# A fused attention and mixture kernel: a second conversion tile, PSUM banks shared 2-3-3, and other order around two units of the second mixture

## The chip, the cores and the metric

The kernel runs on one core of one Trainium2 chip. The core has a matrix engine (TensorE, in the profile PE; its weight loads are the row PEld), three elementwise engines (VectorE or DVE, ScalarE or ACT, GpSimd or POOL), and a sync engine (SP) that here only issues transfers. Each engine works through its own instructions in order and waits on semaphores. The metric is the device time of one execution in microseconds (us); lower is better.

## The reference

All of it is float32. Attention (plain softmax at a quarter of the resolution plus a band of seven keys) gives 2304 rows of 512; then follow two dense blocks:

```python
def _moe_ref(x, w1, w2, w3, w_out):      # 512 -> 768 -> 512
    h = np.maximum(np.maximum(x @ w1, x @ w2), x @ w3)
    return h @ w_out

def _moe2_ref(x, w_a, w_b, w_out):       # 512 -> 1536 -> 512
    a = x @ w_a
    b = x @ w_b
    return a * b @ w_out
```

The weights arrive as float64 bit patterns. This case is about the second block, called the second mixture here.

## The kernel before

**Tiling.** The 2304 rows are six blocks of 384 (`TB`). Every float32 operand is kept as a high part and a low part, and a product is three passes (high by high, low by high, high by low). The second mixture takes its 1536 columns in six chunks `c` of 256 and its rows in three pairs `p` of blocks. A *unit* is one (c, p). The loop over units runs (0,0), (0,1), (1,0), ... (5,1) and then (0,2) to (5,2): units 0 to 11, then 12 to 17. Unit 11, (5,1), is called `turn` in the code.

**A unit** (`m2_unit`, line 878) computes `a` and `b` (index j = 0, 1) for two column tiles and two blocks by a scheme of seven products in place of eight, in the order 1, 2, 6, 5, 7, 4, 3. Each product is done for j = 0 and j = 1, with six matmuls of 384 columns each (`prod`, line 827). Products 1, 6, 7 and 4 accumulate in the two "ua" banks, with a copy out by ACT in between (`snap`, tile `sn`); product 2 takes two "ub" banks, product 5 two more, on which product 3 then accumulates. `m2_done` (line 853) adds a bank to a copy (DVE): for j = 0 into `ca`, for j = 1 into `g`, and multiplies `g` by `ca`. `m2_parts` splits `g` into `gh` (ACT cast, line 874) and `gl` (POOL subtraction, line 875), one step of the unit later.

**Output.** `m2_o` (line 917) multiplies the `g` of the unit before by `w_out`: six steps of six matmuls of 512 columns, each into an "o" bank (`bank`, line 607), each followed by an addition into `acc` (DVE, line 944; in chunk 0 a copy by ACT, line 942) and, in the last chunk, by a store. The main loop sets these *o steps* between the products with `o(n)`: one after product 6, one after 5, two after 7, two after 4; in unit 11 all six stand after product 4. PSUM has eight banks: "ua" 2, "ub" 4, "o" 2.

**Operands.** `sform(p, ...)` (line 681) makes the seven left operands of a pair from the sums of the first block: for each a cast on ACT (line 691), a subtraction (line 694) on DVE where its number is in `SUB_DVE`, else on POOL, and between them differences on DVE (`less`, line 700, in place). It is a generator in lane 0. Pair 0 and 1 are made around the end of the first mixture. The sums of blocks 4 and 5 (pair 2) are written to DRAM in unit 0 (`spill`), and `refill` (line 1056) reads them back into two "w6" tiles at the start of unit 10; `sform(2, ...)` is queued at the start of unit 11.

**Weights.** `convert_steps` (line 463) turns 512 columns of float64 bits into float32 on DVE (lines 471, 474, 479, 481, 488) and ACT (478), with tiles `ce` and `cm` of one buffer each (`CB = 1`). For the rows of `w_out` the result stays in `cm`, from which `split2` (line 764) takes it to `wo` (ACT 768, POOL 770). `conv2_in` and `conv2_out` are generators in lane 1. All split weights are also stored to DRAM, and units 12 to 17 load them again (`load2`, line 818), some on SP's queue and some on ACT's.

**Order.** From the end of attention on the order on each engine is the program's (`manual_schedule`). `tick` runs the lanes, lane 0 first; a lane stops at a yielded tuple such as ("x", 4) until the main loop has put it into `opened`. In an engine's queue a transfer stands where the program issues it. The last lines of the loop's body, where unit n loads `w_out` rows again, are:

```python
        o(6 if turn else 2)
        while prev_o:
            part(one_o)
        opened.add(("o", n - 1))
        if turn:
            load2(nc.scalar, 0, 0, 3)
        elif p == 2:
            load2(nc.scalar, c, 1, 3)
            load2(nc.scalar, c + 1, 0, 3)
        step(3)
```

Of the kernel before, what the change touches and what calls it, by code (L numbers as in the profile page):

```python
# [38 lines left out]
W2B = 4  # L39
SNB = 5  # L40

SUB_DVE = (0, 2, 4)

SUM_ACT = (0, 1, 2, 3, 4, 6, 7, 8, 9, 10, 13, 14, 15)
NORM_POOL = (0, 1, 2, 3, 4, 5, 6, 7, 8, 9, 10, 11, 13, 14, 15)
# [4 lines left out]
def attn_moe_kernel(  # L50
# [397 lines left out]
    W = 12 * P  # L448
    NP_ = 512
    raw, wt = {}, {}  # L450

    def load_piece(key, srcs):

# [9 lines left out]
    def convert_steps(key, w=None):  # L463

        r = raw.pop(key)
        lo, hi = r[:, :, 0], r[:, :, 1]
        top = r.rearrange("p n w -> p (n w)").bitcast(U16).rearrange("p (n w) -> p n w", w=4)[:, :, 3]
        e = rawp.tile([P, NP_], U16, tag="ce", name="ce", bufs=CB)
        m = rawp.tile([P, NP_], U32, tag="cm", name="cm", bufs=CB)
        s16, f = e.bitcast(I16), m.bitcast(F32)  # L470
        nc.vector.tensor_scalar(  # L471
            out=e, in0=top, scalar1=0x7FF0, scalar2=None, op0=ALU.bitwise_and
        )
        nc.vector.tensor_scalar(  # L474
            out=m, in0=hi, scalar1=0x000FFFFF, scalar2=0x00100000, op0=ALU.bitwise_and, op1=ALU.bitwise_or
        )
        yield
        nc.scalar.activation(out=s16, in_=e, func=AF.Relu, bias=ebias, scale=8.0)  # L478
        nc.vector.scalar_tensor_tensor(out=f, in0=lo, scalar=2.0**-32, in1=m, op0=ALU.mult, op1=ALU.add)  # L479
        yield  # L480
        nc.vector.scalar_tensor_tensor(  # L481
            out=e, in0=top, scalar=0x8000, in1=e, op0=ALU.bitwise_and, op1=ALU.bitwise_or
        )
        yield
        out, i0, i1 = f if w is None else w, f, e.bitcast(BF16)
        if w is not None and len(w.shape) == 3:
            i0, i1 = (x.rearrange("p (a b) -> p a b", a=w.shape[1]) for x in (i0, i1))
        nc.vector.scalar_tensor_tensor(out=out, in0=i0, scalar=2.0**-20, in1=i1, op0=ALU.mult, op1=ALU.mult)  # L488
        yield f
# [116 lines left out]

    def bank():
        if 2 in psp_:
            return psp_[2].tile([P, 512], F32, tag="o", name="ps_m", bufs=2)
        return bk("d", "ps_m")  # L610

    def m1_p(c, blk, j):
# [40 lines left out]
            else:  # L653
                nc.vector.tensor_tensor(out=a, in0=ps, in1=a, op=ALU.add)  # L654

    late = {}

# [20 lines left out]
    def sform(p, s0, s1):  # L681


        b11, b21, b12, b22 = (s[:, k * YH : (k + 1) * YH] for s in (s0, s1) for k in range(2))
        n = [0]

        def part(i, w):
            t = ys_tile(p, n[0])
            h = t[:, :HK].rearrange("p k t -> p (k t)")
            l = t[:, HK:].rearrange("p k t -> p (k t)")  # L690
            nc.scalar.copy(h, w)
            yield
            eng = nc.vector if n[0] in SUB_DVE else nc.gpsimd
            eng.tensor_tensor(out=l, in0=w, in1=h.bitcast(F32), op=ALU.subtract)
            n[0] += 1
            ys[p, i] = t
            yield

        def less(o, a, b):
            nc.vector.tensor_tensor(out=o, in0=a, in1=b, op=ALU.subtract)  # L700

        if p == 1:
            yield ("x", 4)
        yield from part(1, b11)
        less(b11, b12, b11)
        yield
        yield from part(2, b21)
        yield from part(5, b11)
        less(b12, b22, b12)
        less(b11, b22, b11)  # L710
        yield
        if p == 0:
            yield ("x", 2)
        if p == 1:
            yield ("x", 5)
        yield from part(7, b12)
        yield from part(6, b11)
        less(b21, b21, b11)
        yield
        yield  # L720
        if p == 1:
            yield ("x", 6)
        yield from part(4, b21)
        if p == 0:
            yield ("x", 3)
        yield from part(3, b22)
# [126 lines left out]
    def m2_done(c, p, j, i, b, ps, t):  # L853

        if j == 0:
            o = ca[i, b] = late["p"].tile([P, TB], F32, tag="ca", name="ca", bufs=2)
            if t is None:
                nc.scalar.copy(o, ps)
            else:
                nc.vector.tensor_tensor(out=o, in0=ps, in1=t, op=ALU.add)  # L860
            return
        g = late["p"].tile([P, TB], F32, tag="g", name="g", bufs=3)
        if t is not None:
            nc.vector.tensor_tensor(out=g, in0=ps, in1=t, op=ALU.add)  # L864
        nc.vector.tensor_tensor(out=g, in0=ps if t is None else g, in1=ca.pop((i, b)), op=ALU.mult)  # L865
        fresh.append((c, p, i, b, g))
# [11 lines left out]
    def m2_unit(c, p):  # L878


        def bank_u(tag, n):
            return psp_[2].tile([P, 512], F32, tag=tag, name="ps_u", bufs=n)[:, :TB]

        A, E, T2 = [None] * 2, [None] * 2, [None] * 2
        T1 = [None] * 2
        for j in range(2):
            A[j] = bank_u("ua", 2)
            prod(A[j], c, p, j, 1, True)
            T1[j] = snap(A[j])
            yield  # L890
        for j in range(2):
            b = bank_u("ub", 4)
            prod(b, c, p, j, 2, True)
            m2_done(c, p, j, 0, 0, b, T1[j])
            yield
        for j in range(2):
            prod(A[j], c, p, j, 6, False)
            T2[j] = snap(A[j])
            yield
        for j in range(2):  # L900
            E[j] = bank_u("ub", 4)
            prod(E[j], c, p, j, 5, True)
            yield
        for j in range(2):
            prod(A[j], c, p, j, 7, False)
            m2_done(c, p, j, 1, 1, E[j], snap(A[j]))
            yield
        for j in range(2):
            prod(A[j], c, p, j, 4, False)
            m2_done(c, p, j, 1, 0, A[j], None)  # L910
            yield
        for j in range(2):
            prod(E[j], c, p, j, 3, False)
            m2_done(c, p, j, 0, 1, E[j], T2[j])
            yield
# [154 lines left out]
    for n, (c, p) in enumerate(units):  # L1070
        unit = m2_unit(c, p)
        turn = (c, p) == (NC2 - 1, 1)

        nxt = c + 1 if p == 2 else 0 if turn else NC2
        if n == 0:
            lanes[1].extend(conv2(*x) for x in conv2_order(0, 0))
        elif p < 2:
            lanes[1].extend(conv2(*x) for x in conv2_order(c, p))
        if (c, p) == (NC2 - 1, 0):
            back = list(refill())  # L1080
        if turn:
            lanes[0].append(sform(2, *back))

        def part(f):
            old, fresh[:] = fresh[:], []
            f()
            for x in old:
                m2_parts(*x)

        def step(m, k_=1):  # L1090
            for _ in range(m):
                part(lambda: next(unit, None))
                tick(k_)

        def one_o():
            while prev_o and next(prev_o[0], StopIteration) is StopIteration:
                prev_o.pop(0)

        def o(m):
            for _ in range(m):  # L1100
                part(one_o)
                tick(2)

        step(4)
        if n == 0:
            m1_o(*last)
            spill(4)
            spill(5)
            acc_ctx.close()
            xps["e"] = ctx.enter_context(tc.tile_pool(name="xpe", bufs=2, side="right", reuse_waits="tile"))  # L1110
            opened.add(("x", 6))
        else:
            prev_o = [m2_o(*u) for u in prev_u]
        if p == 2:
            if c == 0:
                load_in(1, 0)
            load_in(c + 1, 2)
        step(2)
        if p == 1 and c < NC2 - 1:
            opened.add(("a", n, 0))  # L1120
        if turn:
            load2(nc.sync, 0, 0, 0)
        elif p == 2:
            load_in(c + 1, 1)
        if not turn:
            o(1)
        step(2, 2)
        if not turn:
            o(1)
        step(2)  # L1130
        if not turn:
            o(2)
        step(2)
        if p == 1 and c < NC2 - 1:
            opened.add(("a", n, 1))
        if turn:
            load2(nc.scalar, 0, 1, 0)
            load_in(0, 1)
            load_in(0, 2)
        elif p == 2:  # L1140
            load_in(c + 2, 0)
# [10 lines that stand above are left out]
        prev_u = [(c, 2 * p), (c, 2 * p + 1)]  # L1152
# [33 lines left out]
```

## Time and profile before

| | |
|---|---|
| median of 3 runs | 895.41 us (894.58 to 904.71) |
| the profiled execution | 895.55 us, span 893.3 us |
| mean granted TensorE clock | 0.974 |
| PE busy | 853.1 us, 95% of the span |
| PE weight loads | 795.0 us, 89% |
| DVE busy | 620.9 us, 70% |
| ACT busy | 346.4 us, 39% |
| POOL busy | 381.6 us, 43% |
| second mixture, units 0 to 17 | from 449.92 us to the end |

The span goes from the first to the last instruction of the profiled execution; its time has 2.25 us more around it. Times in the rows are counted from the span's start. Matmuls are pipelined: a row's duration covers its latency, so the distance between starts tells how fast they go. The granted clock is 1.00 at 2.4 GHz and 0.50 at 1.2 GHz.

### The profile page before, as it was taken

The numbers are of one execution on the slowest core, as the hardware profiler recorded it, in microseconds if no ns is written. First come the engines' busy times: TensorE is split into PE (matmuls) and PEld (weight loads), VectorE is DVE, ScalarE is ACT, GpSimd is POOL, SyncE is SP. The second block draws the span as 40 slices with busy tenths as digits, with TensorE's granted clock in tenths as the row PEclk, the third lists the DMA queues.
The fourth block names the chain that finished last, engine by engine and source line by source line (L and its number), as shares of the span: only waits on it lengthen the run. The fifth ranks groups of instructions, "written<-read, shape, count | busy, mean of one in ns | idle before, by whom it ended". The sixth has DMA issues, their size and how long they took to land.

```text
span 893.3 us, 14751 instructions
## 1 busy us (share of the span) xinstructions
PE 853.1 (95%) x5590; PEld 795.0 (89%) x5590; DVE 620.9 (70%) x1101; ACT 346.4 (39%) x791; POOL 381.6 (43%) x388
## 2 busy tenths in 40 slices
PE   5899889999999999999987899999999989999998
PEld 4778779999999999999986898898889989999996
DVE  5989996754675685757869788989898564334444
ACT  4576565545422232322333553334334242322221
POOL 5777776644232232323545454455444333111111
PEclk9599989999999999999999999999999999999999
DMA  8875754311121130211315444444443348755612
GB/s 186 187 147 120 141 120 91 77 31 38 50 71 48 38 97 31 77 77 72 130 70 187 167 177 177 156 175 176 150 180 113 135 144 333 254 212 212 212 48 95
DMA packets 125110, 116.22 MB, mean 130 GB/s; under 512 B 81392, under 2 KB 107760, under 8 KB 125040
## 3 DMA queue, kind: packets, MB, share of 16 engines
q1 hardware_dynamic: 120720, 97.98, 36.3%
q10 hardware_dynamic: 4320, 17.30, 5.3%
q8 instruction: 44, 0.72, 0.3%
q14 instruction: 26, 0.21, 0.1%
HBM read 80.66 MB, written 34.60 MB: 129 GB/s over the span
## 4 chain that ended last, share of the span: by engine, by line
PE 73%; DVE 19%; issue 3%; ACT 2%; DMA 2%; POOL 1%; SPq 0%; DVEq 0%; ACTq 0%
PE ps_m L602 44%; PE ps_u L836 19%; PE ps_s L303 3%; DVE ce L471 2%; DVE cm L474 2%; PE ps_av L416 2%; DVE ce L481 2%; DVE g L865 2%; PE ps_sd L295 2%; PE ps_tl L391 1%; DVE F L488 1%; DVE cm L479 1%; DVE acc L944 1%; DVE g L864 1%; PE ps_ud L402 1%
## 5 line engine op out<-in xcount | busy, mean ns | idle before, releaser
L602 PE MATMUL ps_m<-xh,w 128*128 128x384 f32 x864 | 174.8, 340 | 1.4 <-DVE t L631 1.4
L875 POOL TENSOR_TENSOR gl<-g,gh 128x384 fp32r<-128x384 f32 x72 | 75.4, 1048 | 212.9 <-ACT gh L874 197.6
L602 PEld LDWEIGHTS ps_m<-xh,w 128*128 128x128 f32 x864 | 152.1, 190 | 2.4 <-DVE t L631 1.6
L836 PE MATMUL ps_u<-xh,w 128*128 128x384 f32 x720 | 135.7, 338 | 2.4 <-DVE ca L860 1.7
L602 PE MATMUL ps_m<-wo,gh 128*128 128x512 f32 (+1 forms) x436 | 131.2, 395 | 6.3 <-DVE acc L944 3.0
L836 PEld LDWEIGHTS ps_u<-xh,w 128*128 128x128 f32 x720 | 127.9, 190 | 5.5 <-DVE ca L860 2.0
L836 PE MATMUL ps_u<-xl,w 128*128 128x384 f32 x648 | 121.8, 336 | 3.6 <-DVE g L865 1.7
L836 PEld LDWEIGHTS ps_u<-xl,w 128*128 128x128 f32 x648 | 113.9, 188 | 7.0 <-DVE g L865 2.0
L602 PEld LDWEIGHTS ps_m<-wo,gh 128*128 128x128 f32 x436 | 79.9, 188 | 23.7 <-DVE acc L944 6.5
L944 DVE TENSOR_TENSOR acc<-ps_m,acc 128x512 f32<-128x512 f32 (+1 forms) x91 | 61.5, 682 | 56.4 <-PE ps_m L602 56.3
L602 PE MATMUL ps_m<-xl,w 128*128 128x384 f32 x432 | 94.3, 336 | 0.0
L874 ACT CAST gh<-g 128x384 fp32r<-128x384 f32 x72 | 37.0, 514 | 138.1 <-DVE g L865 120.6
L631 DVE TENSOR_TENSOR t<-ps_m,t 128x384 f32<-128x384 f32 x72 | 39.9, 555 | 68.6 <-PE ps_m L602 54.9
L848 ACT COPY sn<-ps_u 128x384 f32<-128x384 f32 x108 | 50.0, 478 | 80.2 <-PE ps_u L836 68.6
L602 PE MATMUL ps_m<-hh,wo 128*128 128x384 f32 x288 | 73.7, 337 | 3.6 <-DVE acc L654 2.1
L602 PEld LDWEIGHTS ps_m<-xl,w 128*128 128x128 f32 x432 | 76.3, 188 | 0.5 <-issue 0.4
L637 POOL TENSOR_TENSOR hl<-t,hh 128x384 fp32r<-128x384 f32 x36 | 36.4, 1010 | 79.2 <-ACT hh L636 77.8
L602 PE MATMUL ps_m<-wo,gl 128*128 128x512 f32 (+1 forms) x218 | 67.8, 392 | 0.0
L481 DVE SCALAR_TENSOR_TENSOR ce<-raw,ce 128x512 uint16<-128x512 uint16 x60 | 50.5, 842 | 18.1 <-ACT ce L478 18.1
L654 DVE TENSOR_TENSOR acc<-ps_m,acc 128x384 f32<-128x384 f32 x120 | 61.4, 552 | 1.1 <-PE ps_m L602 1.1
L478 ACT ACTIVATE ce<-ce,ebias 128x512 int16<-128x512 uint16 x60 | 43.5, 725 | 40.5 <-DVE ce L471 40.3
L860 DVE TENSOR_TENSOR ca<-ps_u,sn 128x384 f32<-128x384 f32 x54 | 29.9, 554 | 40.7 <-PE ps_u L836 21.0
(123 smaller groups left out, 1423.6 us busy)
## 6 DMA issues: line engine op xcount, KB each, us to landing
dw<-w SPq DMA_DIRECT2D x24, 768.0 KB
raw<-in_moe_w_dram SPq DMA_DIRECT2D x18, 512.0 KB
raw<-in_moe_w_out_dram SPq DMA_DIRECT2D x18, 512.0 KB
w<-dw SPq DMA_DIRECT2D x12, 768.0 KB
w<-dw ACTq DMA_DIRECT2D x12, 768.0 KB
dw<-wo SPq DMA_DIRECT2D x12, 512.0 KB
wo<-dw ACTq DMA_DIRECT2D x12, 512.0 KB
vr<-in_v_dram SPq DMA_DIRECT2D x16, 288.0 KB
```

The lines of the kernel that those rows point to most:

```text
L478: nc.scalar.activation(out=s16, in_=e, func=AF.Relu, bias=ebias, scale=8.0)
L481: nc.vector.scalar_tensor_tensor(out=e, in0=top, scalar=0x8000, in1=e, op0=ALU.bitwise_and, op1=ALU.bitwise_or)
L602: nc.tensor.matmul(ps, lhs[a], rhs[b], start=(i == 0), stop=(i == n - 1))
L631: nc.vector.tensor_tensor(out=t, in0=ps, in1=cur["t"], op=ALU.max)
L637: nc.gpsimd.tensor_tensor(out=l, in0=t, in1=h.bitcast(F32), op=ALU.subtract)
L654: nc.vector.tensor_tensor(out=a, in0=ps, in1=a, op=ALU.add)
L836: nc.tensor.matmul(ps, w[:, a, slot, kk], y[:, b * HK + kk], start=start and i == 0, stop=i == 3 * HK - 1, skip_group_check=not start,)
L848: nc.scalar.copy(t, ps)
L860: nc.vector.tensor_tensor(out=o, in0=ps, in1=t, op=ALU.add)
L874: nc.scalar.copy(h, g)
L875: nc.gpsimd.tensor_tensor(out=l, in0=g, in1=h.bitcast(F32), op=ALU.subtract)
L944: nc.vector.tensor_tensor(out=a, in0=ps, in1=a, op=ALU.add)
```

## The change

It does five things; all else keeps its order.

- Conversion: once the pool `late` exists (after attention), every other piece takes its `ce` and `cm` from that pool, so that there are two of each. The buffers of `g` there go from three to two.
- Banks: "ub" has 3 instead of 4, "o" 3 instead of 2; "ua" keeps 2.
- `SUB_DVE` is now set for each pair; for pair 1 only part 2 stays on DVE, parts 0 and 4 go to POOL.
- `sform(2, ...)` is queued in unit 10. It is let go in three steps: ("x", 7) in unit 10 before product 6, ("x", 8) there after product 7, ("x", 9) at the start of unit 11.
- Unit 17 has its o steps two after product 6, two after 5, two after 7.

```diff
-SUB_DVE = (0, 2, 4)
+SUB_DVE = {0: (0, 2, 4), 1: (2,), 2: (0, 2, 4)}
...
+    late, late_n = {}, [0]
...
-        e = rawp.tile([P, NP_], U16, tag="ce", name="ce", bufs=CB)
-        m = rawp.tile([P, NP_], U32, tag="cm", name="cm", bufs=CB)
+        late_n[0] += "p" in late
+        pl = late["p"] if late_n[0] % 2 else rawp
+        e = pl.tile([P, NP_], U16, tag="ce", name="ce", bufs=CB)
+        m = pl.tile([P, NP_], U32, tag="cm", name="cm", bufs=CB)
...
-            return psp_[2].tile([P, 512], F32, tag="o", name="ps_m", bufs=2)
+            return psp_[2].tile([P, 512], F32, tag="o", name="ps_m", bufs=3)
...
-            eng = nc.vector if n[0] in SUB_DVE else nc.gpsimd
+            eng = nc.vector if n[0] in SUB_DVE[p] else nc.gpsimd
...
         if p == 1:
             yield ("x", 4)
+        if p == 2:
+            yield ("x", 7)
         yield from part(1, b11)
...
             yield ("x", 5)
+        if p == 2:
+            yield ("x", 8)
         yield from part(7, b12)
...
             yield ("x", 6)
+        if p == 2:
+            yield ("x", 9)
         yield from part(4, b21)
...
-        g = late["p"].tile([P, TB], F32, tag="g", name="g", bufs=3)
+        g = late["p"].tile([P, TB], F32, tag="g", name="g", bufs=2)
...
-            b = bank_u("ub", 4)
+            b = bank_u("ub", 3)
...
-            E[j] = bank_u("ub", 4)
+            E[j] = bank_u("ub", 3)
...
         if (c, p) == (NC2 - 1, 0):
-            back = list(refill())
+            lanes[0].append(sform(2, *refill()))
         if turn:
-            lanes[0].append(sform(2, *back))
+            opened.add(("x", 9))
...
+        if (c, p) == (NC2 - 1, 0):
+            opened.add(("x", 7))
         step(2)
...
-        if not turn:
-            o(1)
+        end = n == len(units) - 1
+        o(0 if turn else 2 if end else 1)
         step(2, 2)
-        if not turn:
-            o(1)
+        o(0 if turn else 2 if end else 1)
         step(2)
-        if not turn:
-            o(2)
+        if (c, p) == (NC2 - 1, 0):
+            opened.add(("x", 8))
+        o(0 if turn else 2)
         step(2)
```

## Rows read from the trace of the kernel before

**Rows 1.** Windows by stage: from:to, length, busy us (instructions) per engine, PEclk, DMA share, GB/s.

```profile
449.92:502.95 53.03, 43.26 (x217) 39.34 (x217) 38.79 (x59) 23.35 (x44) 27.53 (x22) 0.97 0.38 138
502.95:692.39 189.44, 186.44 (x962) 170.71 (x962) 167.68 (x258) 77.41 (x150) 93.07 (x81) 1.00 0.46 165
692.39:715.38 22.99, 22.99 (x121) 21.38 (x121) 13.41 (x21) 6.46 (x13) 7.42 (x7) 1.00 0.36 130
715.38:742.49 27.11, 24.70 (x123) 22.86 (x123) 17.32 (x23) 10.05 (x18) 11.93 (x8) 0.94 0.53 191
742.49:880.10 137.61, 137.61 (x720) 127.96 (x719) 53.77 (x90) 34.47 (x72) 24.38 (x24) 1.00 0.54 194
880.10:893.30 13.20, 9.25 (x44) 7.18 (x43) 5.42 (x9) 0.51 (x1) 1.01 (x1) 0.94 0.38 141
```

**Rows 2.** Timeline, from unit 5 into 6: start, duration, engine, line, operation, [idle before].

```profile
571.62 2.25 PE L836 MATMUL ps_u<-xh,w 128*128 128x384 f32 x12
573.71 2.26 PE L836 MATMUL ps_u<-xl,w 128*128 128x384 f32 x12
...
573.59 0.55 DVE L860 TENSOR_TENSOR ca<-ps_u,sn 128x384 f32<-128x384 f32 x1
```

**Rows 3.** Timeline of PE, units 0 and 1; in brackets the idle time before.

```profile
457.51 0.62 PE L602 MATMUL ps_m<-hh,wo 128*128 128x384 f32 x2 [2.09 <-DVE acc L654]
...
470.42 2.39 PE L836 MATMUL ps_u<-xh,w 128*128 128x384 f32 x12 [1.67 <-DVE ca L860]
...
477.26 1.31 PE L836 MATMUL ps_u<-xl,w 128*128 128x384 f32 x6 [1.68 <-DVE g L865]
...
494.21 0.73 PE L602 MATMUL ps_m<-wo,gh 128*128 128x512 f32 x2 [2.37 <-ACT acc L942]
```

**Rows 4.** Timelines of DVE and POOL, the end of the first mixture and unit 0.

```profile
445.29 2.49 DVE L700 TENSOR_TENSOR acc<-acc 128x768 f32<-128x768 f32 x1
...
456.04 0.95 DVE L694 TENSOR_TENSOR xl<-acc,xl 128x768 fp32r<-128x768 f32 x1
...
468.74 0.43 DVE L474 TENSOR_SCALAR cm<-raw 128x512 uint32<-128x512 uint32 x1 [7.78 <-POOL wo L770]
...
445.07 1.89 POOL L694 TENSOR_TENSOR xh<-acc,xh 128x768 fp32r<-128x768 f32 x1 [3.51 <-ACT xh L691]
```

**Rows 5.** Windows around three pauses of PE; the column after POOL is its clock.

```profile
459.00:461.00 2.00, 2.00 (x8) 2.00 (x7) 1.76 (x3) 0.00 (x0) 0.00 (x0) 0.50 0.23 95
...
490.00:494.00 4.00, 1.84 (x9) 1.24 (x7) 3.86 (x8) 1.03 (x2) 0.00 (x0) 1.00 0.56 201
...
728.00:730.00 2.00, 1.62 (x5) 1.62 (x6) 1.01 (x2) 1.44 (x3) 1.82 (x1) 0.50 0.00 0
```

**Rows 6.** Waits of PEld, units 2 to 9 (total, times, longest); POOL's group from the page.

```profile
PEld ps_m L602 <- DVE acc L944: 6.2, 10, 0.9
...
L875 POOL TENSOR_TENSOR gl<-g,gh 128x384 fp32r<-128x384 f32 x72 | 75.4, 1048 | 212.9 <-ACT gh L874 197.6
```

**Rows 7.** Timelines of SP, PE, ACT and a window's traffic, units 10 and 11.

```profile
694.79 1.47 SPq L1059 DMA_DIRECT2D w<-y  x2
...
701.00:702.00 1.00, 1.00 (x8) 1.00 (x7) 0.00 (x0) 0.00 (x0) 0.00 (x0) 1.00 0.53 221
...
703.53 2.24 PE L836 MATMUL ps_u<-xl,w 128*128 128x384 f32 x12
...
727.12 0.83 ACT L691 CAST xl<-w 128x768 fp32r<-128x768 f32 x1 [3.50 <-DVE w L700]
...
728.38 3.73 PE L836 MATMUL ps_u<-ys,w 128*128 128x384 f32 x12 [2.41 <-ACT sn L848]
```

**Rows 8.** Timeline of the last unit: ACT, its queue of transfers, and PE.

```profile
876.28 0.51 ACT L874 CAST gh<-g 128x384 fp32r<-128x384 f32 x1 [1.25 <-DVE g L865]
...
878.15 0.33 ACTq L822 DMA_DIRECT2D wo<-dw  x1
...
881.51 0.47 PE L602 MATMUL ps_m<-wo,gh 128*128 128x512 f32 x1 [0.84 <-DMA wo<-dw]
```

More of the change, by code (lines that the diff above doesn't have):

```diff
@@ L654, in m1_o @@
                 nc.vector.tensor_tensor(out=a, in0=ps, in1=a, op=ALU.add)
-    late = {}
     HK = NK // 2
```

## The prediction

> **What bounds the kernel now.** I read the page first: TensorE (PE) is busy for 95% of the span, and in its forty slices the 9s break only at the very start, near slice 20, near slice 32 and at the end. So I cut the span into stages with the table of windows [rows 1]; its borders are starts of units in the chain of work that ended last. A unit here is one (c, p) of the second mixture.
>
> Six units on the third pair last 137.61 us, 22.94 each, with PE busy throughout and the clock at 1.00 [rows 1]. That is the floor of a unit. Twelve matmuls of 384 columns take 2.09 us from start to start (571.62 to 573.71 [rows 2]), 0.174 each; a unit has 84 of them, 14.6 us, so its 36 matmuls of the output, six "o" steps of six, are 22.94 - 14.6 = 8.3 us, 1.39 a step.
>
> Against that floor the stages lose: units 0 and 1 last 53.03 and should need 14.6 (unit 0 has no o steps) + 2.1 (the last `m1_o`, 12 matmuls) + 22.94 = 39.6, so 13.4 is lost; units 2 to 9 last 189.44 against 183.5, 5.9 lost; unit 10 nothing; unit 11 27.11, 4.2 lost; units 12 to 17 nothing; after them come the last six o steps (8.3) in 13.20. All the change can win is here, about 23.5 us, 2.6%. Everything before 449.92 keeps its instructions.
>
> **The start (units 0 and 1).** Four rows of PE's timeline show what it waited for [rows 3]: a bank that VectorE (DVE) had not read (2.09 us), DVE's `ca` (1.67), DVE's `g` (1.68), and a bank that ScalarE (ACT) had not copied (2.37). Behind them [rows 4]:
>
> - Third "o" bank and the moved subtraction. At 457.51 the third of four outputs waited for the first's addition, which DVE made after a 0.95 us subtraction of `sform(1)` (456.04). The diff sends that one to POOL (`SUB_DVE[1]` keeps only part 2), so the addition moves to about 456.05 and ends near 456.65; the third output has a bank of its own, runs to 455.8, and the fourth waits 0.85 instead of the third 2.09: 1.24 won. The pause at 457.51 was followed by a clock of 0.50, the 1.2 GHz level, in 459 to 461 [rows 5]: about 1.0 us lost, which I count as won.
> - The further conversion tile. DVE stood 7.78 us, to 468.74, because the one `cm` tile was still being read by POOL's split (`wo`, L770). With pieces alternating between two `ce`/`cm` pairs, DVE goes on at about 461, and `ca` waits only for its product. The 1.67 at 470.42 goes. The 1.68 at 477.26 stays mostly: DVE works through conversion, `ca`, `g` in one line there, and that line just starts sooner. I take 0.9 of it and its neighbours.
> - At 494.21 the fourth o step waited for ACT's copy of the second, itself behind a conversion step. With three banks it needs the first's copy, long done: 2.37 gone, but the next product needs a `sn` copy from that same ACT line, about 0.5 later: 1.87 won.
> - The price. Part 0's subtraction, also moved to POOL, reads `b11`, which DVE's L700 then overwrites: DVE must now wait for POOL's 1.89 us. At 445.29 an L700 beside POOL's subtraction (445.07) took 2.49 instead of 0.95. Bounds: 0 if DVE's own 0.95 saved pays for it, 1.2 if the L700 also sits out POOL's next subtraction. I take the middle, 0.6.
>
> Start: 1.24 + 1.0 + 1.67 + 0.9 + 1.87 - 0.6 = 6.1 us won. Bounds 2.0 (the last bank wait alone) and 9.0 (all 13.4 but 0.85, 0.5 and some 3 of DVE's line).
>
> On that price the Trainium skill (SBUF — State Buffer, Who interferes with whom) says that a DVE instruction with two SBUF inputs and a POOL instruction that reads SBUF exclude each other for the whole instruction. The 2.49 us row agrees; by that rule alone the price is the full 1.2 and the sum 0.6 us higher.
>
> **Units 2 to 9.** The PE loads waited 6.2 us in ten waits, all for `acc` (L944) to free an "o" bank [rows 6]. With three banks the fifth o step needs the bank of the second, not of the third, whose addition lies more than 2.8 us (two steps) earlier; the longest wait was 0.9. I take 5.4 of 5.9; bounds 2.5 and 5.9, the low one if shorter units let DVE fall behind. The third bank comes from "ub", four to three. Now the second bank of product 2 waits for `ca` of the preceding unit's product 3: in the tightest unit that is read at 573.59 and takes 0.56, while product 2's second half starts 3.1 us after 573.71, less 0.8 for the removed waits: 1.9 us of room [rows 2]. `g` from three to two buffers: a buffer comes back two results later, at the closest (product 4 to the next unit's 2) after three products and two o steps, 3 x 2.09 + 2.78 = 9.05 us, and POOL's split that frees it takes 1.05 [rows 6]; it would have to start 8 us late to matter: nothing.
>
> **Units 10 and 11 (the turn).** In unit 11 PE waited 2.41 us for an ACT `sn` that stood behind `sform(2)`'s copy, itself 3.50 late for DVE [rows 7]; the clock then was 0.50 [rows 5], and 12 matmuls took 3.73. That is the 4.2. The change puts five of the seven operands into unit 10, where DVE is busy 13.41 of 22.99 us [rows 1]; unit 11 keeps two, both subtracted on POOL. What is new: the first ACT copy now wants the refill from DRAM from the middle of product 6 on. The refill is issued at 694.79 as before and the DMA traffic thins out between 701 and 702 [rows 7]; ACT and all queued behind it (the `sn` of product 6's second half, then `gh`) stand until about 701.6, and the second half of product 7 (703.53 plus half of 2.09) needs that `sn` near 704.6. Copy 0.84 and `sn` 0.48 end at 702.9. So 1.7 us of room, and DVE, late too, has a third bank to lean on. I take 3.7 won; bounds 1.5 and 4.2.
>
> **The last unit.** Its o steps go 2-2-2 instead of 1-1-2-2, so the last two precede product 4 (12 matmuls) instead of following it. That moves the issue of the last `wo` load, which the program puts on ACT's queue behind the `gh` cast of product 4. Before, ACT was ready at 876.28 and the load went at 878.15, when the last o step freed the slot; it landed 3.36 us later, at 881.51, and PE waited 0.84 for it [rows 8]. Now the slot is free earlier, but product 4 ends two o steps (2.78) later, so `gh` starts at 879.06 and the load goes then: 0.91 later, and nothing covers it, since PE reaches its own end of products at the same time. So +0.9; PE then stands about 1.8 us. Such a pause cost the clock at 728.38 but a longer one, 2.37, did not: 490 to 494 shows 1.00 [rows 5]. I add 0.4 of a possible 1.5: +1.3, bounds +0.9 and +2.4.
>
> On the clock the Trainium skill (TensorE: Matmul & The Clock Gate, What's actually happening) says that its watching window runs free, so that equal pauses may cost or not. These rows agree; by it the end is +0.9 or +2.4, never between.
>
> **Sum.** -6.1 - 5.4 - 3.7 + 1.3 = -13.9 us. The profiled execution took 895.55 us (span 893.3 and 2.25 around it): 881.65. The median shown is 895.41, 0.14 lower: 881.5 us. Against 895.41 that is -1.55%; about 2% (17.9 us, below 877.5) is what a measurement of this kernel tells from no change.
>
> **Rivals.**
> - *The start's waits only move.* Speaks for it: after 468.74 DVE has hardly an idle row. If `g` and `sn` hold PE as long as before, the start wins 2.0: 885.6, up to 888 if clock losses stay.
> - *DVE becomes the bound in units 2 to 9.* It is busy 167.68 of 189.44 us there [rows 1], and shorter units leave it 91%. If the steady gain is only 0.5: 886.4. Against: its idle rows before o steps show that it catches up in each second unit.
> - *The turn's stall moves to unit 10*, ACT standing for the refill. If the refill lands after 704, product 7 waits and the turn wins 0 to 1.5: 883.7 to 885.2.
> - *Slower: the "ub" banks.* With POOL taking more and DVE converting beside it, DVE's lag at product 3 passes the 1.9 us of room and the wait recurs in all eight units. It outweighs the 13.9 once each waits 1.74 us, a lag of 3.65. With a lag of 4.5 it is 8 x 2.6 = 20.8 - 13.9, 902.3. Against: the tightest lag row already is that of a DVE in a long backlog, and it still leaves the room.
> - *Everything at its bound*: -9.0 - 5.9 - 4.2 + 0.9 = -18.2, 877.2.
>
> **How the numbers follow.** Forecast 62% (878 to 886); start's waits move 14%; DVE the bound 9%; turn 6%; "ub" banks 5%, of it 3 in 100 beyond 913.3 (2% slower: a lag near 5.9); all bounds 4%. Low 877.5 and high 890.0 leave out the last, the "ub" case and the worst mixtures of the three middle ones (all three at once: -2.0 - 0.5 - 1.5 + 2.4, 893.8). Faster by over 2%: 0.05; within: 0.92; slower: 0.03.
>
> **What would show it.** Right: no 7.78 us row at `cm`, unit 2 starting near 497 instead of 502.95; no PE wait on L944 between units 2 and 9, with 46.0 us per two units; unit 11 near 23.3 us without a 0.50 clock and L691 rows in unit 10 near 701; PE waiting about 1.8 us for `wo` before its last o steps. Wrong: PE waits on `ca` or `g` at product 2 or 5 in each unit (the banks), an ACT row idle past 704 for the refill, or units 2 to 9 still over 23.4 us.

## The result and the profile after

The kernel after takes 889.76 us at the median of 20 runs, the kernel before, timed beside it, 896.98. The ratio is 0.9905 with a 95% interval of 0.9879 to 0.9932: some 8.5 us won (6.1 to 10.9), where 13.9 were forecast. The ratio is that of the fast executions alone: six of the 20 after, 894.58 us and more at a lower granted clock, are left out of it, while the medians are of all. The profiled execution took 889.42 us, its span is 887.6.

The windows of the kernel after, cut at the starts of units 0, 2, 10, 11 and 12 and of the last o steps (from:to, length, then busy us and instructions of PE, PEld, DVE, ACT, POOL, then PEclk, DMA share, GB/s):

```profile
451.73:498.02 46.29, 41.36 (x216) 37.85 (x217) 40.15 (x59) 22.62 (x44) 29.36 (x21) 1.00 0.43 154
498.02:685.45 187.43, 185.06 (x961) 171.01 (x961) 174.07 (x258) 78.00 (x152) 95.38 (x82) 1.00 0.46 166
685.45:709.63 24.18, 23.52 (x122) 21.25 (x122) 19.77 (x24) 8.79 (x16) 10.08 (x8) 1.00 0.38 142
709.63:734.35 24.72, 23.65 (x121) 21.23 (x121) 13.99 (x22) 7.51 (x15) 10.27 (x8) 1.00 0.62 218
734.35:872.35 138.00, 138.00 (x722) 128.33 (x721) 53.79 (x90) 34.35 (x72) 23.99 (x24) 1.00 0.53 190
872.35:887.60 15.25, 10.34 (x43) 8.06 (x42) 5.43 (x9) 0.51 (x1) 1.42 (x2) 0.89 0.37 136
```

In [rows 1] two borders lie one matmul off: unit 12 of the kernel before starts at 742.31, not 742.49, and its last o steps at 880.27, not 880.10. Cut at its start, the last stretch of the kernel before is:

```profile
880.27:893.30 13.03, 9.08 (x43) 7.01 (x42) 5.42 (x9) 0.51 (x1) 1.01 (x1) 0.94 0.38 137
```

By these starts a unit on the third pair takes 137.96 / 6 = 22.99 us; that is the floor, not the 22.94 of the prediction, and eight units take 183.9. The table takes the same starts for both kernels (us):

| stage | before | after | won | forecast |
|---|---|---|---|---|
| units 0 and 1 | 53.03 | 46.29 | 6.74 | 6.7 (and a price of 0.6, which falls ahead of unit 0) |
| units 2 to 9 | 189.44 | 187.43 | 2.01 | 5.4 |
| units 10 and 11 | 49.92 | 48.90 | 1.02 | 3.7 |
| units 12 to 17 | 137.96 | 138.00 | -0.04 | 0 |
| last o steps | 13.03 | 15.25 | -2.22 | -1.3 |

The start came out as forecast, two stages won far less, and the end lost more. What precedes unit 0 took 1.81 us longer in this execution; that length differs from run to run (unit 0 starts between 444.62 and 454.11 in most of the runs below), so I compare stages.

The timeline of PE, units 0 and 1 of the kernel after, its waits in brackets; these answer [rows 3]:

```profile
451.73 2.37 PE L843 MATMUL ps_u<-xh,w 128*128 128x384 f32 x12 [1.24 <-DVE acc L657]
458.92 0.61 PE L605 MATMUL ps_m<-hh,wo 128*128 128x384 f32 x2 [1.17 <-DVE acc L657]
...
474.15 1.31 PE L843 MATMUL ps_u<-xl,w 128*128 128x384 f32 x6 [1.71 <-DVE g L872]
...
490.96 2.35 PE L843 MATMUL ps_u<-ys,w 128*128 128x384 f32 x12 [0.83 <-ACT sn L855]
```

The wait of 2.09 us for the "o" bank is 1.17 (0.85 forecast), the 1.67 for `ca` is gone with DVE's 7.78 us idle row [rows 4], the 1.68 for `g` stands as it was, and in place of the 2.37 for ACT's copy there are 0.83 for the `sn` copy behind it (0.5 forecast). The clock was 1.00 throughout.

In units 2 to 9 the waits of PE changed their name. The waits table of the kernel after in that stage (total us, times, longest), against 6.2 us for `acc` in [rows 6]:

```profile
PEld ps_u L843 <- ACT sn L855: 3.3, 3, 1.1
PE ps_u L843 <- ACT sn L855: 2.4, 3, 0.8
...
PEld ps_m L605 <- DVE acc L951: 0.4, 2, 0.2
```

Cut by unit, the windows of the kernel after show where (unit 4, then unit 5; 6 and 8 are like 4, 7 and 9 like 5):

```profile
544.11:567.10 22.99, 22.99 (x121) 21.32 (x121) 21.00 (x29) 8.24 (x16) 13.00 (x11) 1.00 0.53 206
567.10:591.21 24.11, 23.30 (x122) 21.34 (x122) 23.03 (x38) 10.31 (x20) 10.50 (x10) 1.00 0.39 132
```

Unit 4 is at the floor of 22.99. Unit 5 is over it by 1.1 us, and DVE is busy 23.03 of its 24.11 us, with 38 instructions against 29 in unit 4. At its border with unit 4 the chain is this (timelines of DVE, ACT and PE of the kernel after):

```profile
570.08 1.15 DVE L872 TENSOR_TENSOR g<-g,ca 128x384 f32<-128x384 f32 x1
...
571.31 0.51 ACT L881 CAST gh<-g 128x384 fp32r<-128x384 f32 x1 [2.33 <-DVE g L872]
571.73 0.85 ACT L855 COPY sn<-ps_u 128x384 f32<-128x384 f32 x2
...
572.26 2.02 PE L843 MATMUL ps_u<-xl,w 128*128 128x384 f32 x10 [0.81 <-ACT sn L855]
```

DVE, late, delivers `g` (this multiplication of two operands in SBUF runs beside a POOL subtraction, 569.52 to 570.81, and takes 1.15 us; with POOL idle it takes 0.56); ACT has stood 2.33 us for it with the cast `gh`; the `sn` copy that PE needs stands behind that cast on ACT.

DVE also needed longer for the same work: 174.07 us against 167.68 [rows 1], with 258 instructions in both. The groups of the conversion's `cm` step (24 instructions, busy us, mean ns), from the lines view of DVE in that stage. The kernel before:

```profile
L474 DVE TENSOR_SCALAR cm<-raw 128x512 uint32<-128x512 uint32 x24 | 15.7, 656 | 0.0
```

The kernel after:

```profile
L477 DVE TENSOR_SCALAR cm<-raw 128x512 uint32<-128x512 uint32 x24 | 24.0, 1000 | 0.0
```

That is 8.3 us more in one line. One such instruction takes 0.42 us, or 1.0 to 1.5 when it starts while a POOL subtraction runs; the long form came 7 times in 24 before and 16 times after. Two of them, and POOL's row beside the long one, from the timelines of the kernel after:

```profile
563.45 1.19 POOL L882 TENSOR_TENSOR gl<-g,gh 128x384 fp32r<-128x384 f32 x1 [1.04 <-ACT gh L881]
563.68 1.24 DVE L477 TENSOR_SCALAR cm<-raw 128x512 uint32<-128x512 uint32 x1
...
571.49 0.42 DVE L477 TENSOR_SCALAR cm<-raw 128x512 uint32<-128x512 uint32 x1
```

At the turn, ACT, DVE, POOL and PE of units 10 and 11 of the kernel after:

```profile
695.01 0.84 ACT L692 CAST xh<-w 128x768 fp32r<-128x768 f32 x1 [1.43 <-DMA w<-y]
...
697.03 1.84 POOL L695 TENSOR_TENSOR xl<-w,xl 128x768 fp32r<-128x768 f32 x1 [2.37 <-ACT xl L692]
697.36 2.33 DVE L701 TENSOR_TENSOR w<-w,w 128x768 f32<-128x768 f32 x1
699.71 0.83 ACT L692 CAST xh<-w 128x768 fp32r<-128x768 f32 x1 [2.76 <-DVE w L701]
...
706.05 0.73 PE L605 MATMUL ps_m<-wo,gh 128*128 128x512 f32 x2 [0.46 <-DVE acc L951]
715.34 4.50 PE L843 MATMUL ps_u<-xl,w 128*128 128x384 f32 x24 [0.88 <-ACT sn L855]
```

The refill did what was forecast: ACT's first cast starts 9.6 us into unit 10 (9.2 forecast) and PE does not stand for it. Then DVE's L701 takes 2.33 us beside POOL's subtraction, ACT stands 2.76 us for it, and DVE's additions come late: unit 10 is 24.18, unit 11 24.72, where 22.94 and some 23.3 were forecast.

The end of the kernel after, ACT, its queue and PE:

```profile
871.16 0.51 ACT L881 CAST gh<-g 128x384 fp32r<-128x384 f32 x1 [1.25 <-DVE g L872]
871.17 0.33 ACTq L829 DMA_DIRECT2D wo<-dw  x1
...
874.58 0.49 PE L605 MATMUL ps_m<-wo,gh 128*128 128x512 f32 x1 [1.83 <-DMA wo<-dw]
875.72 1.91 PE L605 MATMUL ps_m<-wo,gh 128*128 128x512 f32 x4
```

The load went 0.01 us after `gh` started, PE waited 1.83 us (1.8 forecast), and behind the pause the clock fell: four matmuls took 1.91 us where the same four take 1.09 later in that stretch.

### The profile page after: what moved, and what is told of

Read it like the earlier page. It is cut to its first block, busy times and chain, and to the rows that moved or that the text cites. A ratio compares the mean times of both kernels' runs of the same rounds, so it can differ in the third digit from the quotient of the medians.

```text
span 887.6 us, 14751 instructions
## 1 busy us (share of the span) xinstructions
PE 853.3 (96%) x5590; PEld 796.0 (90%) x5590; DVE 629.6 (71%) x1099; ACT 346.9 (39%) x791; POOL 388.6 (44%) x390
## 4 chain that ended last, share of the span: by engine, by line
PE 78%; DVE 13%; issue 3%; DMA 2%; ACT 2%; SPq 1%; POOL 1%; DVEq 0%; ACTq 0%; POOLq 0%
PE ps_m L605 46%; PE ps_u L843 22%; PE ps_s L303 2%; PE ps_av L416 2%; DVE ce L484 2%; DVE g L872 2%; PE ps_tl L391 1%; PE ps_sd L295 1%; DVE cm L477 1%; PE ps_ud L402 1%; PE ps_td L381 1%; DVE acc L951 1%; DVE cm L482 1%; DMA w<-y 1%; DVE ce L474 1%
```

## The experiments

The first four change the kernel before and have a ratio from ten runs; of the others only the last has one. Where no ratio is given the kernel ran once, so its stages are read and not its whole time. A stage that an edit leaves alone differs from run to run too: units 2 to 9 took 187.07 to 187.44 us in four runs that keep that stage of the kernel after, unit 10 23.97 to 24.24.

**The bank sharing alone.**

```diff
-            return psp_[2].tile([P, 512], F32, tag="o", name="ps_m", bufs=2)
+            return psp_[2].tile([P, 512], F32, tag="o", name="ps_m", bufs=3)
...
-            b = bank_u("ub", 4)
+            b = bank_u("ub", 3)
...
-            E[j] = bank_u("ub", 4)
+            E[j] = bank_u("ub", 3)
```

> The kernel before with the banks alone shared 2-3-3. Own theory (the third "o" bank removes PE's waits for an "o" bank, but in every second unit DVE is late and the wait comes back at product 6, through ACT's queue): units 0 and 1 lose the 2.37 us wait and a part of the 2.09, so 50 us instead of 53.0; units 2 to 9 fall from 189.4 to about 187.6; units 10 and 11 stay at 50.1; together about -5 us. Rival (the bank alone would win all 5.9 us in units 2 to 9, and it is the conversion tile or the two g buffers that gave it back): units 2 to 9 last 184 us, together about -8.5 us.

Ratio 0.9926 (0.9899 to 0.9954). The profiled execution was a long one (904.52 us), but its clock was 1.00 from unit 0 to unit 9. Units 0 and 1 took 49.61 us, 3.1 less than the 52.76 and 52.74 of the two runs below that leave this stage alone. Units 2 to 9 took 189.05, nothing less than the 188.67 to 189.44 of three runs without a change there. So the third "o" bank does not shorten the steady stage by itself: PE's loads waited 2.7 us for `acc` and 4.2 for `sn` in place of 6.2 for `acc`. The stages account for some 3 us, less than the interval of the ratio (4.1 at the least); the rest is not settled.

**The conversion tile alone** (with `g` at two buffers).

```diff
+        late_n[0] += "p" in late
+        pl = late["p"] if late_n[0] % 2 else rawp
-        e = rawp.tile([P, NP_], U16, tag="ce", name="ce", bufs=CB)
-        m = rawp.tile([P, NP_], U32, tag="cm", name="cm", bufs=CB)
+        e = pl.tile([P, NP_], U16, tag="ce", name="ce", bufs=CB)
+        m = pl.tile([P, NP_], U32, tag="cm", name="cm", bufs=CB)
...
-        g = late["p"].tile([P, TB], F32, tag="g", name="g", bufs=3)
+        g = late["p"].tile([P, TB], F32, tag="g", name="g", bufs=2)
```

> The kernel before with the second conversion tile and two g buffers alone. Own theory (it acts only where DVE stood for POOL's split of cm, in units 0 and 1): the 7.78 us idle row is gone, units 0 and 1 last about 50 us instead of 53.0, units 2 to 9 stay at 189.4 within 0.5, units 10 and 11 at 50.1; together -3 us. Rival (conversion that runs beside POOL's work makes DVE slower): units 2 to 9 take 191 us or more, with more than 170 us of DVE busy there against 167.7, and the sum is 0.

Ratio 0.9970 (0.9924 to 1.0015): no difference that can be told. Units 0 and 1 took 51.63 us, 1.1 less; PE's pause just ahead of unit 0 fell from 0.72 to 0.26. Units 2 to 9 took 187.53, 1.1 to 1.9 less than without it, which I had not put down to this part: the steady stage's whole gain in the kernel after is there with the tile alone. The waits for `acc` were still 4.0 us, and DVE was busy less than before, 163.06 us against 167.68; its `ce` step alone fell from 18.8 to 13.1 us. The window of units 2 to 9 with the tile alone:

```profile
496.25:683.78 187.53, 185.74 (x962) 170.75 (x961) 163.06 (x258) 77.84 (x150) 92.46 (x81) 1.00 0.46 164
```

**The third pair's operands begun sooner, alone.**

```diff
-            back = list(refill())
+            lanes[0].append(sform(2, *refill()))
...
-            lanes[0].append(sform(2, *back))
+            opened.add(("x", 9))
```

(with the three stops "x" 7, 8 and 9 as in the change)

> The kernel before with the third pair's operands begun in unit 10 alone. Own theory (the stall of unit 11 moves to unit 10: the operands start when the refill has landed, and DVE, held by POOL's subtraction, is late with the additions that free the "o" banks): units 10 and 11 last 48.5 to 50 us against 50.1, with waits for "o" banks in unit 10 that are longer than with three of them; together -0.5 to -1.5 us. Rival (the refill is what is late, and two banks are enough): 47 us or less, -3 us, with no wait for a bank.

Ratio 0.9995 (0.9959 to 1.0032). The windows of unit 10 and unit 11:

```profile
692.63:719.90 27.27, 24.80 (x121) 22.52 (x121) 21.67 (x28) 10.13 (x18) 11.02 (x9) 0.94 0.30 110
719.90:742.91 23.01, 23.01 (x121) 21.35 (x121) 11.31 (x16) 6.59 (x13) 7.72 (x6) 1.00 0.67 234
```

From the timeline of PE, the one wait of PE in unit 10:

```profile
709.89 1.22 PE L602 MATMUL ps_m<-wo,gh 128*128 128x512 f32 x2 [2.48 <-DVE acc L950]
```

Unit 11 is cured, unit 10 has all of the stall, with the slow clock behind it. It is the order of DVE that does it: the addition that frees the "o" bank stands behind the subtractions and L700s of the third pair. With two "o" banks, moving the work sooner only moves the stall.

This run leaves units 0 and 1 as they were. Its clock there, behind PE's wait of 2.35 us for ACT's copy in unit 1:

```profile
495.00:497.00 2.00, 2.00 (x7) 1.78 (x6) 1.97 (x5) 0.10 (x1) 0.73 (x1) 0.50 0.73 236
```

**The last unit's order alone.**

```diff
-        if not turn:
-            o(1)
+        end = n == len(units) - 1
+        o(0 if turn else 2 if end else 1)
         step(2, 2)
-        if not turn:
-            o(1)
+        o(0 if turn else 2 if end else 1)
```

> The kernel before with only the last unit's order changed. Own theory (the last load of wo is issued behind the cast of product 4's result, 0.9 us later than before, and PE's pause of some 1.8 us may lower the clock): from the end of the last product to the end of the span 14.1 us with the clock kept or about 15.3 with a clock of 0.50, against 13.2; +0.9 to +2.1 us. Rival (it is the other parts that delay this load): 13.2 us, no difference.

Ratio 1.0037 (0.9995 to 1.0078). The window of the last o steps:

```profile
882.14:896.20 14.06, 9.09 (x43) 7.01 (x42) 5.42 (x9) 0.51 (x1) 1.42 (x2) 1.00 0.40 147
```

PE's wait in it, from its timeline:

```profile
884.38 0.47 PE L602 MATMUL ps_m<-wo,gh 128*128 128x512 f32 x1 [1.84 <-DMA wo<-dw]
```

The pause is that of the kernel after to 0.01 us, the clock kept, and the stretch is 14.06 against 13.03 in the kernel before: +1.0.

**After, with a unit's last casts held.** The cast `gh` and the subtraction `gl` of a unit's last product are issued one step later, behind the next unit's `sn` copies.

```diff
-            old, fresh[:] = fresh[:], []
+            old, fresh[:] = held + fresh, []
+            held[:] = []
...
+            if hold:
+                held[:] = old
+                return
...
-        step(4)
+        step(4, h=(0,))
...
-        step(3)
+        step(3, h=(2,))
```

> The changed kernel, but the split of a unit's last product (gh, gl) is issued after the sn copies of the next unit's product 1 instead of before them. Own theory (what is left in units 2 to 9 is ACT standing for DVE's late g, with the sn copies that PE needs for product 6 queued behind): the waits of PE on sn go, units 2 to 9 fall from 187.4 to about 184.3 us, units 3, 5, 7, 9 (24.1 each where they were slow) to 23.1 or less, and unit 11 from 24.9 to about 23.8; together -4 us. Rival (DVE itself is the bound in every second unit, so PE then waits for g or ca at product 2 or for acc): units 2 to 9 stay above 186.5 and the waits change their name.

Units 2 to 9 took 187.11 us, 0.3 less, which is no more than runs without this edit differ. The waits in that stage:

```profile
PEld ps_m L605 <- DVE acc L951: 3.9, 5, 1.3
PE ps_m L605 <- DVE acc L951: 2.2, 3, 0.8
```

The wait for `sn` is gone and the one for `acc` is back in its place. So the cast that stands ahead of `sn` is not the cause in the steady stage; it is where a late DVE is felt first. In unit 11 it was the cause of most: 24.72 became 23.50.

**After, with pair 1's subtractions back on DVE.**

```diff
-SUB_DVE = {0: (0, 2, 4), 1: (2,), 2: (0, 2, 4)}
+SUB_DVE = {0: (0, 2, 4), 1: (0, 2, 4), 2: (0, 2, 4)}
```

> The changed kernel, but pair 1's parts 0 and 4 are subtracted on DVE as before. Own theory (the move frees DVE when the last m1_o needs its additions, and costs about 0.5 us by POOL's subtraction that DVE must wait for): PE's pause before unit 0 falls from 1.24 to about 0.7 us, and units 0 and 1 last about 47.5 us against 46.3, since DVE's line is 0.95 later at the last m1_o; net +0.7 us. Rival (the move is the greater part of what the start won): units 0 and 1 last 48.5 us or more.

Units 0 and 1 took 47.18 us, 0.89 more. But PE's pause just ahead of unit 0, which is outside that window, is 0.25 us here and 1.24 in the kernel after:

```profile
454.11 2.35 PE L843 MATMUL ps_u<-xh,w 128*128 128x384 f32 x12 [0.25 <-DVE acc L657]
462.17 0.62 PE L605 MATMUL ps_m<-hh,wo 128*128 128x384 f32 x2 [2.06 <-DVE acc L657]
```

What moving the subtractions wins at the last output of the first mixture (2.06 to 1.17) it pays, 0.99, ahead of unit 0: in sum 0.1 us, nothing.

**After, with the third pair's second operand subtracted on DVE.**

```diff
-SUB_DVE = {0: (0, 2, 4), 1: (2,), 2: (0, 2, 4)}
+SUB_DVE = {0: (0, 2, 4), 1: (2,), 2: (0, 1, 2, 4)}
```

(the numbers count the operands in the order in which they are made, from 0, so that the second one changes engine)

> The changed kernel, but part 2 of the third pair (the second operand) is subtracted on DVE instead of POOL. Own theory (in unit 10 DVE is late by its own work on the operands, of which 1.4 us is L701 held beside POOL's subtraction: 2.33 us instead of 0.95): that L701 takes 0.95, the second pair of L701 ends about 1 us sooner, the waits for an "o" bank in unit 10 (0.5 and 0.9) go, and units 10 and 11 last 48 us or less against 49.1. Rival (the refill alone sets it, or DVE's 0.96 more of work eats the gain): 49.1 us or more.

The windows of units 10 and 11:

```profile
680.70:703.69 22.99, 22.99 (x121) 21.38 (x121) 19.48 (x25) 8.79 (x16) 8.23 (x7) 1.00 0.40 149
703.69:728.18 24.49, 23.62 (x121) 21.24 (x121) 13.75 (x21) 7.52 (x15) 10.27 (x8) 1.00 0.64 221
```

The L701 that took 2.33 us in the kernel after, from the timeline of DVE:

```profile
692.55 0.95 DVE L701 TENSOR_TENSOR w<-w,w 128x768 f32<-128x768 f32 x1
```

Without POOL's subtraction beside it the L701 takes 0.95, and unit 10 is at the floor, although DVE has one instruction more. The loss of unit 10 was that meeting of DVE and POOL.

**After, casts held, and the conversion's sums moved to POOL.**

```diff
-        tt(nc.vector, 3, 7, 5, ALU.add)
+        tt(nc.gpsimd, 3, 7, 5, ALU.add)
...
-        tt(nc.vector, 2, 3, 0, ALU.subtract)
+        tt(nc.gpsimd, 2, 3, 0, ALU.subtract)
```

> After, with the casts of a unit's last g held back by one step (as in the experiment that held them) and, new, with both float32 sums of the conversion steps of w_a and w_b (the line of F) taken from VectorE to GpSimd: about 1 to 2 us of VectorE's work less in each of units 2 to 9. Own theory, VectorE's load bounds the units 2 to 9: VectorE's busy time there falls from about 174 us to 160 or less, and 2 to 9 shorten from 187.1 us to 185.5 or less (floor 183.5), with the waits for acc under 2 us. Rival, VectorE is not what bounds (GpSimd or the port that both use takes its place): 2 to 9 stay at 187 us or more; GpSimd's sums make VectorE's two-operand additions longer, and PE waits for acc, sn or gl as long as before.

Units 2 to 9 took 189.33 us, 2.2 more, with DVE at 166.09 busy. The timelines of ACT and DVE show why this does not decide the question:

```profile
565.50 1.57 ACT L775 CAST w<-F 128x768 fp32r<-128x768 f32 x2 [5.35 <-POOL F L788]
...
567.48 0.56 DVE L867 TENSOR_TENSOR ca<-ps_u,sn 128x384 f32<-128x384 f32 x1 [3.68 <-ACT sn L855]
```

ACT stood 5.35 us for POOL's sums, with PE's `sn` copies behind it, and DVE stood for those. A new wait took the place of the load that was removed.

**After, casts held, and the conversion's sums cut from 256 to 16 columns** (part of the sums is left out, so less work is done; one `F` tile is kept throughout instead of a new one for each piece).

```diff
-            eng.tensor_tensor(out=F[:, o], in0=F[:, a], in1=F[:, b], op=op)
+            w_ = KH if eng is nc.gpsimd or c == 0 else 16
+            eng.tensor_tensor(out=F[:, o, :w_], in0=F[:, a, :w_], in1=F[:, b, :w_], op=op)
...
-        F = late["p"].tile([P, 8, KH], F32, tag="F", name="F", bufs=1)
+        if "F" not in late:
+            late["F"] = late["p"].tile([P, 8, KH], F32, tag="F", name="F", bufs=1)
+        F = late["F"]
```

> After with the casts held, and VectorE's two float32 sums of each conversion (the line of F) cut from 256 to 16 of their columns from the second chunk on, in one F tile kept throughout: part of the sums is left out, so that VectorE has some 0.5 us less to do in each of the 16 such sums of units 2 to 9, about 8 us of 174, and nothing is put on another engine. Own theory, VectorE's load bounds units 2 to 9: 2 to 9 fall from 187.1 to 185.5 us or less (floor 183.5) and PE's waits for acc from 3.9 (with 2.2 of the matmuls themselves) to under 2 in all. Rival, VectorE's total is not what counts (the wait is set by single stands of VectorE on another engine, as in the run with GpSimd): 2 to 9 stay within 0.5 us of 187.1.

The window of units 2 to 9:

```profile
496.99:681.05 184.06, 184.06 (x961) 171.33 (x961) 159.81 (x258) 78.84 (x152) 95.12 (x82) 1.00 0.47 172
```

From the waits table of that stage, DVE's own wait for PE:

```profile
DVE acc L954 <- PE ps_m L605: 9.0, 11, 1.3
```

184.06 us, the floor of 183.9 to 0.2; PE has no idle time in it. DVE was busy 14.1 us less than with the casts held alone: 4.0 of that in the cut sums (9.9 to 5.9), 6.6 in the `cm` step, which came beside POOL 8 times in 24. And DVE now waits 9.0 us for PE's banks, where in the kernel after it never does. So DVE's time is what bounds the units 2 to 9 there.

**After, with the last load on SP's queue.**

```diff
-            load2(nc.scalar, c, 1, 3)
+            load2(nc.sync if end else nc.scalar, c, 1, 3)
```

> After, with the last unit's last load of an output weight issued on SP's queue in place of ACT's, all else as it was. Own theory, the load in after was late only because it stood behind ACT's cast gh: the load now goes when the sixth-last o step frees its slot, before the products 4 and 3 of 2.1 us each and more, lands some 3.4 us later and ahead of its use; no wait of PE for wo, no clock drop, the last stretch falls from 15.25 to 12.2 us (under both 13.02 of before and 15.25), the whole to about 886.5 us. Rival, the slot itself is free late or SP's queue is held: the load is issued under 3.4 us before its use, PE waits over 0.8 us and the stretch stays over 13 us.

The window of the last o steps:

```profile
866.87:878.50 11.63, 8.58 (x43) 7.02 (x42) 5.43 (x9) 0.51 (x1) 1.44 (x2) 0.96 0.37 137
```

The load, from the timeline of SP's queue:

```profile
862.67 0.32 SPq L829 DMA_DIRECT2D wo<-dw  x1
```

The load goes 4.2 us ahead of the last o steps (862.67 to 866.87), PE does not wait, and the stretch is 11.63 against 15.25: 3.6 us. The order of the last unit was good; it was the queue behind the cast that made it cost.

**The three together:** casts held, the second operand on DVE, the last load on SP's queue.

> After, with three of the found losses mended together: the casts of a unit's last g held one step, the third pair's part 2 subtracted on VectorE, and the last load of an output weight on SP's queue. Own theory, the four stages are independent, so the gains add: units 0 and 1 46.3 us, 2 to 9 about 187.1, unit 10 22.99, unit 11 about 23.2, the last stretch about 12.2; against after that is -0.3 -1.2 -1.7 -3.0, some 6 us: 883 us at the median, ratio to before 0.984. Rival, they are not: the held casts and the subtraction moved to VectorE meet in units 10 and 11 and one of these loses what it won alone (10 and 11 together 48 us or more), or the end keeps its wait; then under 3 us are won and the ratio is 0.987 or more.

882.29 us at the median of 6 runs, ratio to the kernel before 0.9835 (0.9792 to 0.9878), where the kernel after has 0.9905 (0.9879 to 0.9932): the lowest of all ratios here. (It was timed beside the kernel before, not beside the kernel after, and whether it passes 2% its interval leaves open.) Its windows of units 10, 11 and the end:

```profile
680.99:703.98 22.99, 22.99 (x121) 21.32 (x121) 19.38 (x25) 9.05 (x16) 8.32 (x7) 1.00 0.40 149
703.98:727.45 23.47, 23.32 (x122) 21.34 (x121) 13.58 (x21) 7.62 (x15) 10.22 (x8) 1.00 0.68 237
...
865.45:877.10 11.65, 8.57 (x43) 7.00 (x42) 5.43 (x9) 0.51 (x1) 1.43 (x2) 1.00 0.37 136
```

From unit 0 on it is 6.4 us shorter than the kernel after: 0.04 + 0.32 + 1.19 + 1.25 + 0.00 + 3.60, by stage. The single edits won 0.36 and 1.22 (casts held), 1.19 and 0.23 (second operand) and 3.62 (SP's queue), 6.6 in sum, so the gains add up.

## Why the prediction was right, and where its sizes were off

The forecast said no difference beyond 2%, and 881.5 us within 877.5 to 890.0; the median of 889.76 lies 0.24 us inside the upper edge. As runs of one kernel lie up to 17 us apart, that it came out just inside is luck; 8.5 us were won of the 13.9. The start and the end went by the mechanisms forecast; the steady stage and the turn, 9.1 us of the forecast, gave 3.0.

- **The start, right in sum.** The two runs that leave the start as it was (the third pair's operands alone, the last unit's order alone) have a pause of 0.72 ahead of unit 0 and 52.75 in units 0 and 1; the kernel after has 1.24 and 46.29. That is 5.94 us won, against 6.1. PE's pauses of over 0.3 us in the two units fell from 9.75 to 4.93 us, 4.8 won where the terms for them made 5.7. The clock, counted as 1.0, was worth more: 0.97 on the mean of 53.03 us before [rows 1] is some 1.6 us by my estimate, and after it was 1.00. It was not peculiar to the one execution. The two other runs have a stretch at 0.50 as well, only in unit 1, behind waits of 2.35 and 2.37 us, and not in unit 0. So one error made up for the other. What such a stretch costs is not fixed: the run with the casts held has one too, at 472 to 474, and took 46.25 us, since its pauses were 1.35 us shorter. The third bank with the conversion tile wins more than the two alone: 6.0 with both (the run with the subtractions back), 3.1 and 1.6 singly, the pause counted. With the tile alone, two pauses of 2.56 and 1.85 us were left, with the clock at 0.50 behind each.
- **The price of the moved subtraction, mis-sized.** L701 took 2.58 us beside POOL, as the row of before had shown for L700 [rows 4]. I took 0.6 of at most 1.2 and it was 0.99. The rule of the Trainium skill (SBUF — State Buffer, Who interferes with whom) that the two exclude each other for the whole instruction would have given 1.2, the estimate made by it in the prediction, which is nearer.
- **Units 2 to 9, the term that failed: 5.4 forecast, 2.0 measured.** The step was that PE's waits for `acc` are a matter of banks and go with a third. They went, from 6.2 to 0.4, and came back as waits for `sn`; with the casts held they were waits for `acc` again. By the prediction's own sign, units still over 23.4 us, this step was wrong: they took 23.43 on the mean. The rival that DVE becomes the bound was right in its mechanism: of its gain of 0.5 and ours of 5.4, the 2.0 is nearer to the rival's. Against it I had held that DVE catches up in each second unit. It does, in the units 4, 6 and 8; in 5, 7 and 9 it is all but full, and a third bank carries no work over to another unit. I had also taken DVE's 167.68 us as fixed. The same 258 instructions took 163.06 us with the tile alone, 171.19 with the banks alone and 174.07 with both. The difference is meetings with POOL: against the shortest of their kind the instructions that overlap one of POOL's lost 27.6, 35.8 and 39.7 us (31.6 before), all others under 1 us in each kernel. With the sums cut it was 28.2, from 39.5 with the casts held alone, so more of that run's relief was fewer meetings with POOL than work left out. Of the 24 `cm` steps 7 were long before, 9 with the tile alone, 8 with the banks alone and 16 with both: neither part alone made that step so long, the two together did. That relieving DVE brings the floor is shown by the run with the cut sums; which share of it the longer `cm` steps have was not separated.
- **The turn: 3.7 forecast, 1.0 measured.** The rival that the stall moves to unit 10 was right in its place and wrong in its cause, the refill. I had priced the meeting of an L700 with POOL's subtraction in the start and overlooked that the same pair stands in the turn. With that meeting taken away unit 10 is at the floor. Of unit 11's excess of 1.7 us, 1.2 went with the casts held. Alone this part won nothing; that it was the third bank that it lacked there is argued from the wait for `acc`, not tried.
- **The last unit: 1.3 forecast, 2.2 measured, within its bounds.** Load, wait and length of the pause came as worked out; the clock was the open part. Of two pauses of 1.83 and 1.84 us the one cost the clock and the other did not, as the Trainium skill has it (TensorE: Matmul & The Clock Gate, What's actually happening: the watching window runs free). So a single run comes out near one bound, +1.0 with the clock kept, or near the other, +2.2 with it lost, and a mean of the two describes neither.
- **The "ub" banks** never showed: no wait of PE for `ca` or for a product's bank appears in the steady stage of the kernel after.

## What to carry to other kernels

A wait for a bank tells where a late engine is felt, not what makes it late; before giving it another buffer, cut the stage into its periods and look at the busy time of the engine that frees the bank in the fullest one. When work is moved to another engine or another time, ask what will run beside it there: the same instruction took three times as long beside POOL. A load issued on a computing engine's queue goes no sooner than the instructions ahead of it, so one that a new order leaves uncovered belongs on a queue that has nothing else to do.

## What the runs showed of the hardware that was not expected

- VectorE's `TENSOR_SCALAR` from and to SBUF, 128 x 512 of uint32, took 0.42 us alone in units 2 to 9 and 1.0 to 1.5 us when it started while POOL ran a subtraction, although it has only one operand in SBUF. Where it starts first it keeps its 0.42 us (at 618.62 in the kernel after, POOL's subtraction from 618.99). The Trainium skill (SBUF — State Buffer, Who interferes with whom) names it among the operations that can take the ports shared with GpSimd, and then exclude it; the rows agree with that.
- The 258 instructions of VectorE in units 2 to 9 took 163.06 to 174.07 us in four kernels with none of them changed; what differs is how many ran beside POOL and for how long.
- VectorE's sum `F` over 16 columns instead of 256 takes 0.17 us instead of 0.42, and beside POOL's subtraction, when that started first, 0.53 to 0.60 instead of 0.78 to 0.85: the wait for POOL does not shrink with the instruction.
- Six runs with the new order of the last unit had PE wait for the load on ACT's queue, 1.83 to 2.38 us. In three of them the low clock followed (last stretch 15.25 to 15.75 us), in three it did not (13.8 to 14.1); a pause of 1.83 us stands on the one side and one of 1.84 on the other.
